# One operand of VectorE's attention products moved to PSUM, z projected alone, a table loaded early and 56 small products ahead of TensorE's list, with every engine's order planned anew

## The chip, the cores and the metric

The kernel runs on one core of a Trainium2 chip. A core has TensorE (matrix products, called PE in the profile, with its weight loads as PEld), VectorE (DVE), ScalarE (ACT), GpSimd (POOL) and SyncE (SP, which issues most loads), on-chip memory SBUF and the accumulator memory PSUM in eight banks. Each engine works through its own list of instructions in order and waits on semaphores for the others. The metric is device time of one execution in microseconds. Before the change it is 243.72 us, the median of three runs (243.62 to 244.6).

## The reference

Four batches of four heads with 1088 positions of 32 features go through linear attention, and the 4352 tokens of 128 features that come out go through a two-layer block. Cut to what is computed:

```python
def phi(x):                                   # S1, S2: 8 x 32
    a = einsum('rd,bhsd->bhsr', S1, x)
    b = einsum('rd,bhsd->bhsr', S2, x)
    return einsum('bhsi,bhsj->bhsij', a, b).reshape(..., 64)
q_p, k_p = phi(q), phi(k)
kv = einsum('bhsf,bhsd->bhfd', k_p, v)
z = sum(k_p, axis=2)
x = einsum('bhsf,bhfd->bhsd', q_p, kv) / (einsum('bhsf,bhf->bhs', q_p, z)[..., None] + 1e-06)
h = tokens(x) @ w_in                          # 128 -> 2048
g = where(h >= 1, h, where(h <= -1, 0, (h + 1) ** 2 / 4))
out = g @ w_out                               # 2048 -> 128
```

S1, S2, w_in and w_out are given in double precision, the rest in single.

## The kernel before

**The two-layer block.** The 4352 tokens are cut in nine chunks of 512 columns (the last has 256), the 2048 inner features in 16 tiles of 128. One chunk and one tile make a unit: 144 of them. `unit(u)` makes h in one PSUM bank by three products (L796 to L798: high part of the weights with high and low part of x, low part with the high part; all in the rounded single format that TensorE takes in one pass), ScalarE makes s = ((h + 1) / 2 clamped at 0) squared (L811, L813), VectorE clamps: g = min(max(h, 1), s) (L816). Then g is split: g_hi is g rounded (a second clamp on VectorE, L816, or a copy on ScalarE, L823, shared out by the table `HI_ACT`), g_lo = g - g_hi is GpSimd's (L827) or, for units that the tables name, VectorE's, with g in a PSUM bank. Three products add the unit to the chunk's accumulator (L837, L838, L841). A "direct" unit (table `FP`) leaves the split out: g itself is multiplied with unrounded weights in one two-pass product (L844). The weights arrive as double-precision words and are rebuilt and split by ScalarE, GpSimd and VectorE (`weights`, `from_double`).

**The attention.** Batch 0 is the front: before its x exists no unit can run. Its k, q and v come first. `keys(0)` projects k (L527), copies to SBUF, forms the products a x b on VectorE or GpSimd (kp, L537), sums them for z (L546), brings z back into the projection's weights as extra columns (L556, L559: the copy into `proj`) and accumulates kv (L567). `queries(0)` projects q with these columns (abq, L656), so that a, b and the share of the denominator come out together; VectorE makes the denominator, its reciprocal, the scaled a (ap) and the products (qp, L682); TensorE turns them (tp, L693), copies bring them to SBUF (qt) and L711 multiplies with kv: nd, of which x_hi and x_lo are made (L443, L444, L723).

Batches 1 to 3 go another way, between the units. `keys(b)`: two banks of projections (abk, L486), two 32 x 32 transposes by VectorE into SBUF (kab, L492), the products kp from kab alone (L505) on VectorE or GpSimd as the table `KP_POOL` says, z (L512), z brought back (L556, L559), kv (L567). `queries(b)`: sixteen products into four banks (abq, L612, with the z columns among the weights), four transposes (qab, L617), all_terms = a x z part (L620), den (L622), the reciprocal (L624), ap (L626), the products qp in three groups (L637, VectorE or GpSimd by `QP_POOL`), their transposes (qt, L642), and gather16 (nd, L737).

**What sets the order.** The program builds a list of steps with a due number, an engine, a cost and the tiles that they read and write; `Plan.run` goes through model time and gives each free engine the step that is due first, holding PSUM banks (`ps`, eight) and SBUF buffers as the table `rings` allows. The result is written out as the order of every engine's list. Until model time `WARM` (24) TensorE's empty places are filled with products of ones (warm, L314 and L315). The numbers at the head of the file (`KEYS`, `QEND`, `FQ`, `I0` and so on) are due numbers and shares.

## Time and profile before

| what | before |
| --- | --- |
| median of three runs | 243.72 us (243.62 to 244.6) |
| the profiled execution | 245.77 us, its span 244.0 us |
| TensorE busy | 231.1 us, 1844 products |
| VectorE busy | 209.0 us, 372 instructions |
| ScalarE busy | 197.2 us, 403 |
| GpSimd busy | 196.3 us, 175 |
| granted TensorE clock, mean | 0.985 |

The span runs from the first to the last instruction. Rows of a timeline are: start in us, length in us, engine, line, operation, what it writes and reads, shape, how many, and in square brackets the idle time before it with what ended it. Rows of a grouped view end with the busy time, the mean length of one in ns, and the idle time before with its causes. Rows of the windows give the stretch, its length, busy time and count of PE, PEld, DVE, ACT and POOL, then the granted TensorE clock, the share of the DMA engines' time and GB/s.

### The profile page before, as it was taken

What the parts mean: (1) busy time and instruction counts of PE and PEld (TensorE: products, weight loads), DVE (VectorE), ACT (ScalarE), POOL (GpSimd) and SP (SyncE); (2) the same over time, 40 slices, a digit from 0 to 9 for tenths busy, and PEclk for the clock granted to TensorE, in tenths of its full rate; (3) what the DMA queues carried; (4) which work ended last, traced back from release to release, by engine and by line L of the source; (5) the groups of instructions that cost most, each with busy time, mean ns of one, the idle gap of its engine ahead of it and who ended that gap; (6) DMA issues with size and microseconds to landing.
All of it is one profiled execution on the core that took longest, in us unless ns stands there. A gap on an engine that the chain in (4) does not pass through costs nothing.

```text
span 244.0 us, 5120 instructions
## 1 busy us (share of the span) xinstructions
PE 231.1 (95%) x1844; PEld 174.7 (72%) x1844; DVE 209.0 (86%) x372; ACT 197.2 (81%) x403; POOL 196.3 (80%) x175
## 2 busy tenths in 40 slices
PE   8879979989999999996999999989999999999994
PEld 3656748757677887574777788767788888888883
DVE  2868889999986999999979999998788588859882
ACT  2548899999989999336588868898899699689993
POOL 5448789997562998986996768999897989969991
PEclk9979999999999999999799999999999999999999
DMA  6971888000001100001000010000100100010001
GB/s 208 415 316 23 261 307 337 6 1 0 0 3 43 43 3 3 0 3 43 3 0 3 0 43 3 1 1 0 47 0 0 42 4 0 1 43 4 0 0 64
DMA packets 4776, 13.88 MB, mean 57 GB/s; under 512 B 528, under 2 KB 784, under 8 KB 4752
## 3 DMA queue, kind: packets, MB, share of 16 engines
q1 hardware_dynamic: 4320, 12.78, 14.4%
q10 hardware_dynamic: 432, 0.79, 0.9%
q8 instruction: 14, 0.23, 0.4%
q14 instruction: 10, 0.08, 0.1%
HBM read 11.34 MB, written 2.23 MB: 56 GB/s over the span
## 4 chain that ended last, share of the span: by engine, by line
PE 61%; DVE 15%; ACT 10%; issue 6%; POOL 5%; DMA 1%; POOLq 0%; ACTq 0%
PE acc L837 9%; PE acc L841 9%; PE acc L838 8%; PE h L796 8%; PE h L797 8%; PE h L798 8%; DVE g L816 5%; ACT s L813 4%; ACT s L811 3%; DVE g_hi L816 3%; POOL g_lo L827 3%; PE acc L844 3%; PE nd L737 2%; POOL kp L505 2%; PE kv L567 2%
## 5 line engine op out<-in xcount | busy, mean ns | idle before, releaser
L827 POOL TENSOR_TENSOR g_lo<-g,g_hi 128x512 fp32r<-128x512 f32 (+1 forms) x128 | 159.0, 1275 | 28.4 <-ACT g_hi L823 12.9
L816 DVE SCALAR_TENSOR_TENSOR g<-h,s 128x512 f32<-128x512 f32 (+1 forms) x135 | 86.1, 649 | 18.4 <-ACT s L813 14.1
L811 ACT ACTIVATE s<-h 128x512 f32<-128x512 f32 (+1 forms) x144 | 78.8, 573 | 15.3 <-PE h L798 12.0
L813 ACT ACTIVATE s<-s 128x512 f32<-128x512 f32 (+1 forms) x144 | 84.7, 614 | 1.8
L816 DVE SCALAR_TENSOR_TENSOR g_hi<-h,s 128x512 fp32r<-128x512 f32 (+1 forms) x91 | 59.2, 654 | 1.7 <-PE acc L838 1.1
L796 PE MATMUL h<-x_hi,wi_hi 128*128 128x512 f32 (+1 forms) x144 | 56.5, 393 | 1.8 <-ACT proj L559 1.3
L797 PE MATMUL h<-x_lo,wi_hi 128*128 128x512 f32 (+1 forms) x144 | 55.1, 383 | 0.0
L798 PE MATMUL h<-x_hi,wi_lo 128*128 128x512 f32 (+1 forms) x144 | 54.9, 381 | 0.0
L837 PE MATMUL acc<-g_hi,wo_hi 128*128 128x512 f32 (+1 forms) x135 | 54.0, 402 | 0.7 <-DVE g_hi L816 0.6
L841 PE MATMUL acc<-g_lo,wo_hi 128*128 128x512 f32 (+1 forms) x135 | 49.0, 393 | 2.3 <-POOL g_lo L827 2.2
L838 PE MATMUL acc<-g_hi,wo_lo 128*128 128x512 f32 (+1 forms) x135 | 51.2, 380 | 0.0
L796 PEld LDWEIGHTS h<-x_hi,wi_hi 128*128 128x128 f32 x144 | 27.1, 189 | 10.0 <-ACT proj L559 1.6
L841 PEld LDWEIGHTS acc<-g_lo,wo_hi 128*128 128x128 f32 x135 | 25.1, 189 | 9.9 <-POOL g_lo L827 3.9
L837 PEld LDWEIGHTS acc<-g_hi,wo_hi 128*128 128x128 f32 x135 | 25.3, 188 | 9.3 <-DVE g_hi L816 2.0
L798 PEld LDWEIGHTS h<-x_hi,wi_lo 128*128 128x128 f32 x144 | 27.2, 189 | 5.5
L797 PEld LDWEIGHTS h<-x_lo,wi_hi 128*128 128x128 f32 x144 | 27.2, 189 | 5.4 <-issue 0.5
L823 ACT CAST g_hi<-g 128x512 fp32r<-128x512 f32 (+1 forms) x44 | 25.4, 582 | 6.7 <-DVE g L816 5.1
L838 PEld LDWEIGHTS acc<-g_hi,wo_lo 128*128 128x128 f32 x135 | 25.4, 188 | 5.1 <-issue 1.0
L505 POOL TENSOR_TENSOR kp<-kab 128x1280 f32<-128x1280 f32 (+1 forms) x4 | 9.9, 2494 | 0.9 <-DVE kab L492 0.9
L844 PE MATMUL acc<-gd,o 128*128 128x512 f32 x18 | 9.1, 598 | 1.1 <-DVE gd L816 1.1
L637 DVE TENSOR_TENSOR qp<-ap,qab 128x768 f32<-128x768 f32 x6 | 9.7, 1611 | 0.1
L642 DVE STREAM_TRANSPOSE qt<-qp 128x768 f32<-128x768 f32 x9 | 8.6, 959 | 0.0
(101 smaller groups left out, 191.1 us busy)
## 6 DMA issues: line engine op xcount, KB each, us to landing
raw_i<-in_w_in SPq DMA_DIRECT2D x4, 512.0 KB, 4.7
raw_o<-in_w_out SPq DMA_DIRECT2D x4, 512.0 KB, 6.6
outT<-o SPq DMA_DIRECT2D x8, 256.0 KB, 2.0
k<-in_kT SPq DMA_DIRECT2D x3, 576.0 KB, 6.6
v<-in_v SPq DMA_DIRECT2D x3, 576.0 KB, 7.6
q<-in_qT SPq DMA_DIRECT2D x3, 576.0 KB, 6.9
k<-in_kT SPq DMA_DIRECT2D x1, 320.0 KB, 3.8
v<-in_v SPq DMA_DIRECT2D x1, 320.0 KB, 6.2
```

The source lines that it names most:

```text
L796: nc.tensor.matmul(t[:, :n], lhsT=wi_hi[:, fj], rhs=x_hi[:, xs], start=True, stop=False)
L797: nc.tensor.matmul(t[:, :n], lhsT=wi_hi[:, fj], rhs=x_lo[:, xs], start=False, stop=False)
L798: nc.tensor.matmul(t[:, :n], lhsT=wi_lo[:, fj], rhs=x_hi[:, xs], start=False, stop=True)
L811: plan.add(u, "ACT", act(n), lambda: nc.scalar.activation(of(s)[:, :n], of(h)[:, :n], AF.Relu, bias=0.5, scale=0.5), r=[h], w=[s])
L813: plan.add(u, "ACT", act(n, False), lambda: nc.scalar.activation(of(s)[:, :n], of(s)[:, :n], AF.Square), w=[s])
L816: nc.vector.scalar_tensor_tensor(out=of(out)[:, :n], in0=of(h)[:, :n], scalar=1.0, in1=of(s)[:, :n], op0=ALU.max, op1=ALU.min)
L823: plan.add(u, "ACT", act(n, False), lambda: nc.scalar.copy(of(g_hi)[:, :n], of(g)[:, :n]), r=[g], w=[g_hi])
L827: plan.add(u, "DVE" if late else "POOL", dve(n) if late else pool_t(n), lambda: eng.tensor_tensor(out=of(g_lo)[:, :n], in0=of(g)[:, :n], i ...
L837: nc.tensor.matmul(of(acc)[:, :n], lhsT=wo_hi[:, fj], rhs=of(g_hi)[:, :n], start=first, stop=False)
L838: nc.tensor.matmul(of(acc)[:, :n], lhsT=wo_lo[:, fj], rhs=of(g_hi)[:, :n], start=False, stop=False)
L841: nc.tensor.matmul(of(acc)[:, :n], lhsT=wo_hi[:, fj], rhs=of(g_lo)[:, :n], start=False, stop=last)
L844: nc.tensor.matmul(of(acc)[:, :n], lhsT=of(whole[j // JW])[:, j % JW * P : (j % JW + 1) * P], rhs=of(g)[:, :n], start=first, stop=last)
```

## The change

1. **One operand in PSUM (batches 1 to 3).** Where VectorE forms kp, ScalarE first copies the b half of kab back into the first projection's PSUM bank, and VectorE reads it there. For the queries the third transpose writes the z part into that bank, where the denominator's product reads it; the reciprocal goes there too, and for groups whose product is VectorE's the scaled a is also written there (per group now, three small products in place of one). The bank is held until the last of these products.
2. **z projected alone.** The queries use the keys' projection weights (eight products into two banks) and four more products into a third bank for the z part, with z's weights in a small tile of their own (`back_z`). The second `proj` tile and the short product of L556 are gone for these batches.
3. **ScalarE's table first.** A copy of 32 columns of ones stands first on ScalarE's list, ahead of the copies that wait for S.
4. **56 tiny products.** They lead TensorE's list (`JUNK`, `count_up`).
5. **The planner** counts TensorE's entries (`rec`), and holds a step back where its model says that the list beyond entry 449 + 256 k is not there yet; the cost of a 32 x 32 transpose is other; all numbers of the tables are other. So the order of every engine's list is another from the first row to the last. There are 12 direct units in place of 9, GpSimd has 121 of the g_lo subtractions in place of 128, VectorE 73 of the g_hi clamps in place of 91 and ScalarE 59 of the copies in place of 44.
6. SBUF places: two small pads, x_hi and x_lo rounded up to whole chunks, and a pool of their own for s, g, g_hi, g_lo and o.

```diff
-FP = (0.24, 0.25, 0.36, 0.36)
+FP = (0.85, 0.78, 0.03, 0)
+JUNK = 56
-KP_POOL = ((0, 2), (1, 0), (1, 1), (2, 1), (3, 0))
+KP_POOL = ((0, 0), (0, 2), (1, 0), (1, 1), (2, 1), (3, 1))
-QP_POOL = ((0, 0), (0, 2), (1, 0), (2, 0), (2, 1))
+QP_POOL = ((0, 0), (1, 0), (1, 1), (1, 2), (2, 1))
-HI_ACT = (0.68, 0.72, 0, 0.27)
+HI_ACT = (0.58, 0.41, 0.49, 0.38)
...
+    HELD, BLOCK = 449, 256
...
+                if e == "PE":
+                    was, told = told, told + s.rec
+                    for k in range((was - self.HELD) // self.BLOCK + 2):
+                        fetched.setdefault(k, now + (6.0 if now < 16 else 2.6))
+                    k = (told - self.HELD) // self.BLOCK
+                    if (was - self.HELD) // self.BLOCK < k:
+                        rest = (told - self.HELD - self.BLOCK * k) / s.rec
+                        cost = max(cost, fetched.setdefault(k, now + 2.6) - now + rest * cost)
...
 def turned32(n):
-    return 0.07 + 0.00116 * n
+    return 0.156 + 0.00105 * n
...
+            if any((b, gi) not in KP_POOL for gi in range(2)):
+                plan.add(d(0.12), "ACT", act(NTL * HR, False), lambda: nc.scalar.copy(
+                    of(abs_[0])[:, : NTL * HR], of(kab)[:, 1].rearrange("p t h i -> p (t h i)")),
+                    r=[kab.part(0), kab.part(1)], w=[abs_[0].part("b")])
...
-                def products(eng=eng, grp=grp, n=n):
+                def products(eng=eng, grp=grp, n=n, pool=pool):
                     x = [of(kab)[:, c, grp[0] : grp[-1] + 1].rearrange("p t h i -> p (t h) i") for c in range(2)]
+                    if not pool:
+                        x[1] = of(abs_[0])[:, grp[0] * HR : (grp[-1] + 1) * HR].rearrange("p (m i) -> p m i", i=R)
...
-            for c0, n in ((0, HR), (HR, R)):
+            for c0, n in ((0, HR), (HR, R))[: 2 if front else 1]:
                 nc.tensor.matmul(of(z)[:, 64 + c0 : 64 + c0 + n], lhsT=back, rhs=of(zm)[:, :n], start=True, stop=True)
 
-        plan.add(d(0.5), "PE", ZB, zback, r=[zm, "back"], w=[z]).mode = 0
-        plan.add(d(0.55), "ACT", act(40), lambda: nc.scalar.copy(
-            proj[b % 2][:, :, 2 * R : 3 * R], of(z)[:, 64 : 64 + HR + R].rearrange("p (h i) -> p h i", i=R)),
-            r=[z], w=[("proj", b % 2)])
+        plan.add(d(0.5), "PE", ZB, zback, r=[zm, "back"], w=[z]).kind(0, 8)
+        if front:
+            plan.add(d(0.55), "ACT", act(40), lambda: nc.scalar.copy(
+                proj[:, :, 2 * R : 3 * R], of(z)[:, 64 : 64 + HR + R].rearrange("p (h i) -> p h i", i=R)),
+                r=[z], w=["proj"])
+        else:
+            plan.add(d(0.55), "ACT", act(HR), lambda: nc.scalar.copy(back_z[:, b % 2], of(z)[:, 64 : 64 + HR]),
+                     r=[z], w=[("back_z", b % 2)])
...
             nm = NTL * H
...
+            abq = [bank(f"abq{b}_{k}") for k in range(2)]
+            cq = bank(f"cq{b}")
+            qab = Buf("kab", f"qab{b}", [P, 2, NTL, H, R])
             den = Buf("dens", f"den{b}", [P, 2 * D, 1])
             ap = Buf("aps", f"ap{b}", [P, nm, R])
...
+            both = [qab.part(0), qab.part(1)]
+            flat = lambda c: of(qab)[:, c].rearrange("p t h i -> p (t h) i")
+            kept = lambda: of(abq[0])[:, : nm * R].rearrange("p (m i) -> p m i", i=R)
+            rec = lambda: of(abq[0])[:, nm * R : nm * (R + 1)].rearrange("p (m i) -> p m i", i=1)
+
+            def project8():
+                for k, rows in enumerate((slice(0, F), slice(F, 2 * F))):
                     for c in quarters:
...
+                        nc.tensor.matmul(of(abq[k])[c, : NTL * D].rearrange("p (t f) -> p t f", f=D),
+                                         lhsT=s_pair[rows, k * D : (k + 1) * D], rhs=of(qb)[rows, :, c],
+                                         start=True, stop=True)
+
+            def project_z():
+                for c in quarters:
+                    nc.tensor.matmul(of(cq)[c, : NTL * D].rearrange("p (t f) -> p t f", f=D),
+                                     lhsT=back_z[:, b % 2], rhs=of(qb)[:, :, c], start=True, stop=True)
+
+            plan.add(d(-0.1), "PE", KPR, project8, r=[qb, "s_pair"], w=abq).kind(2, 32)
+            for k in range(2):
+                plan.add(d(0.0), "DVE", turned32(NTL * D), lambda k=k: nc.vector.transpose(
+                    out=of(qab)[:, :, :, 2 * k : 2 * k + 2].rearrange("p c t h i -> p t c (h i)"),
+                    in_=of(abq[k])[:, : NTL * D].rearrange("p (t c x) -> p t c x", c=2, x=2 * R)),
+                    r=[abq[k]], w=[qab.part(k)])
+            plan.add(d(0.0), "PE", QPR, project_z, r=[qb, ("back_z", b % 2)], w=[cq]).kind(1, 16)
+            plan.add(d(0.1), "DVE", turned32(NTL * D), lambda: nc.vector.transpose(
+                out=of(abq[0])[:, : nm * R], in_=of(cq)[:, : NTL * D]), r=[cq, *both], w=[abq[0].part("c")])
             plan.add(d(0.15), "DVE", dve(nm * R), lambda: nc.vector.tensor_tensor(
...
+                out=all_terms[:, :, :R], in0=flat(0), in1=kept(), op=ALU.mult),
+                r=[*both, abq[0].part("c")], w=["all_terms"])
             plan.add(d(0.2), "DVE", dve(nm * 9), lambda: nc.vector.tensor_reduce(
                 out=of(den)[:, :nm], in_=all_terms, axis=AX.X, op=ALU.add), r=["all_terms"], w=[den])
...
+            plan.add(d(0.25), "DVE", 0.35, lambda: nc.vector.reciprocal(out=rec(), in_=of(den)[:, :nm]),
+                     r=[den], w=[abq[0].part("r")])
             for gi, grp in enumerate(QGRP[b]):
                 d = dues[gi]
                 n = len(grp)
                 g = slice(grp[0] * H, (grp[-1] + 1) * H)
...
                 pool = (b, gi) in QP_POOL
                 eng = nc.gpsimd if pool else nc.vector
+                scaled = (lambda g=g: of(ap)[:, g]) if pool else (lambda g=g: kept()[:, g])
+                tok = ap.part(gi) if pool else abq[0].part(("ap", gi))
+                plan.add(d(0.3), "DVE", dve(n * HR), lambda scaled=scaled, g=g, n=n: nc.vector.tensor_tensor(
+                    out=scaled(), in0=flat(0)[:, g], in1=rec()[:, g].broadcast_to([P, n * H, R]), op=ALU.mult),
+                    r=[*both, abq[0].part("r")], w=[tok])
+                qp = Buf("qp", f"qp{b}_{gi}", [P, 3, H * F])
                 plan.add(d(0.4), "POOL" if pool else "DVE", pool_b(n * H * F) if pool else dve(n * H * F),
...
+                         lambda qp=qp, n=n, g=g, eng=eng, scaled=scaled: eng.tensor_tensor(
                     out=of(qp)[:, :n].rearrange("p t (h i j) -> p (t h) i j", h=H, i=R),
...
+                    in0=scaled().unsqueeze(3).broadcast_to([P, n * H, R, R]),
+                    in1=flat(1)[:, g].unsqueeze(2).broadcast_to([P, n * H, R, R]), op=ALU.mult),
+                    r=[*both, tok], w=[qp])
...
+    plan.add(-44, "ACT", 1.4, lambda: nc.scalar.copy(table, singles[:, :D]), w=["table"])
+
+    def count_up():
+        for _ in range(JUNK):
+            nc.tensor.matmul(of(warm)[:D, :R], lhsT=singles[:, :D], rhs=singles[:, :R], start=True, stop=True)
+
+    plan.add(-60, "PE", 0.05 * JUNK, count_up).kind(0, 4 * JUNK)
```

Three places of the new order. The first is TensorE's list from batch 0's z (`z0`) to its last query product (`abq0`, in four groups; `kv0` is the accumulation of its keys' products, warm are the filling products of ones). Before:

```order
L556 MATMUL z0_196<-zm0_231,back_98 128x32
L556 MATMUL z0_196<-zm0_231,back_98 128x8
L315 LDWEIGHTS const-bfloat16-1.0
L315 MATMUL warm_103<-const-bfloat16-1.0 128x256
L567 MATMUL kv0_240<-kp0_192,v0_112 32x64 x12
L656 MATMUL abq0_1_255<-proj0_99,q0_108 32x96 x8
L656 MATMUL abq0_0_265<-proj0_99,q0_108 32x96 x8
L567 MATMUL kv0_240<-kp0_192,v0_112 32x64 x12
L656 MATMUL abq0_3_294<-proj0_99,q0_108 32x96 x8
L567 MATMUL kv0_240<-kp0_192,v0_112 32x64 x12
L656 MATMUL abq0_2_328<-proj0_99,q0_108 32x96 x12
```

and now:

```order
L584 MATMUL z0_240<-zm0_284,back_102 128x32
L584 MATMUL z0_240<-zm0_284,back_102 128x8
L599 MATMUL kv0_292<-kp0_236,v0_168 32x64 x12
L702 MATMUL abq0_1_307<-proj_103,q0_165 32x96 x8
L702 MATMUL abq0_0_317<-proj_103,q0_165 32x96 x8
L702 MATMUL abq0_3_328<-proj_103,q0_165 32x96 x8
L702 MATMUL abq0_2_343<-proj_103,q0_165 32x96 x12
L599 MATMUL kv0_292<-kp0_236,v0_168 32x64 x12
```

The four groups of query products stand together now, ahead of the second group of kv; ahead of all this the list has the 56 products of ones more.

The second is GpSimd's list where batch 2's queries (`qp2`) and batch 3's keys (`kp3`) come among the units' subtractions (`g_lo`, with the unit's number). Before:

```order
L827 TENSOR_TENSOR g_lo50_1589<-g50_1505,g_hi50_1529 128x512
L505 TENSOR_TENSOR kp3_1607<-kab3_1591 128x1280
L637 TENSOR_TENSOR qp2_0_1631<-ap2_1624,qab2_1556 128x768
L827 TENSOR_TENSOR g_lo51_1648<-g51_1533,g_hi51_1603 128x512
L827 TENSOR_TENSOR g_lo52_1663<-g52_1629,g_hi52_1637 128x512
L637 TENSOR_TENSOR qp2_1_1678<-ap2_1624,qab2_1556 128x768
L827 TENSOR_TENSOR g_lo53_1700<-g53_1661,g_hi53_1668 128x512
```

and now:

```order
L873 TENSOR_TENSOR g_lo50_1599<-g50_1569,g_hi50_1588 128x512
L684 TENSOR_TENSOR qp2_1_1617<-ap2_1610,qab2_1514 128x768
L873 TENSOR_TENSOR g_lo49_1634<-g49_1549,g_hi49_1612 128x512
L873 TENSOR_TENSOR g_lo51_1648<-g51_1603,g_hi51_1629 128x512
L873 TENSOR_TENSOR g_lo52_1677<-g52_1651,g_hi52_1665 128x512
L873 TENSOR_TENSOR g_lo53_1692<-g53_1658,g_hi53_1663 128x512
L873 TENSOR_TENSOR g_lo54_1707<-g54_1675,g_hi54_1682 128x512
L873 TENSOR_TENSOR g_lo55_1721<-g55_1702,g_hi55_1710 128x512
L873 TENSOR_TENSOR g_lo56_1743<-g56_1718,g_hi56_1735 128x512
L533 TENSOR_TENSOR kp3_1766<-kab3_1740 128x1024
L873 TENSOR_TENSOR g_lo57_1785<-g57_1750,g_hi57_1768 128x512
L873 TENSOR_TENSOR g_lo58_1819<-g58_1762,g_hi58_1787 128x512
```

Batch 3's keys stood ahead of batch 2's two query products; now seven units' subtractions lie between, and one of batch 2's query products is left on GpSimd in place of two.

The third is ScalarE's list where batch 1's z goes back into the projection's weights (`proj1` before, `back_z` now; s are the units' two passes). Before:

```order
L811 ACTIVATE s4_647<-h4_581 128x512
L425 CAST wi_hi_89<-magi1_497 128x512
L813 ACTIVATE s4_647<-s4_647 128x512
L811 ACTIVATE s5_663<-h5_625 128x512
L559 COPY proj1_100<-z1_448 128x5x8
L811 ACTIVATE s6_674<-h6_641 128x512
L813 ACTIVATE s5_663<-s5_663 128x512
```

and now:

```order
L465 COPY qt0_413<-tp0_2_0_509 128x384
L592 COPY back_z_104<-z1_481 128x32
L465 COPY qt0_413<-tp0_2_1_522 128x384
L415 ACTIVATE mago1_553<-raw_o1_338 128x512
L447 CAST wo_hi_95<-o32_0_551 128x512
L465 CAST x_hi_97<-nd0_2_0_555 128x3x64
L465 CAST x_hi_97<-nd0_3_0_572 128x2x64
L465 CAST x_hi_97<-nd0_3_1_574 128x64
L857 ACTIVATE s0_612<-h0_582 128x512
```

The copy of z stands ahead of the first unit's s now (s0), and between the sixth and the seventh unit's before (s5, s6).

139 lines of the change are left out of this document (61 added, 78 removed).

## The prediction

> **What bounds the kernel now.** I read the page's busy times first, then TensorE's timeline row by row for starts that lie too far apart, then what the late engine did just before each of them.
>
> ```profile
> span 244.0 us, 5120 instructions
> PE 231.1 (95%) x1844; PEld 174.7 (72%) x1844; DVE 209.0 (86%) x372; ACT 197.2 (81%) x403; POOL 196.3 (80%) x175
> ...
> 84.75 0.39 PE L796 MATMUL h<-x_hi,wi_hi 128*128 128x512 f32 x1
> ...
> 88.91 0.39 PE L796 MATMUL h<-x_hi,wi_hi 128*128 128x512 f32 x1
> ```
>
> TensorE sets the time. From 84.75 to 88.91 lie three units' worth of work, 18 wide products in 4.16 us: 0.231 us from start to start. The busy figure of 95% hides the idle time, since a matmul's modelled length (0.39) is longer than its pitch. The 144 units need six products each (the last 16 at half width): (128 x 6 + 16 x 3) x 0.231 = 188 us. So some 56 us of the span are the start, the attention work of batches 1 to 3 on TensorE, the end, and gaps. The gaps show in the timeline:
>
> ```profile
> 31.30 0.40 PE L841 MATMUL acc<-g_lo,wo_hi 128*128 128x512 f32 x1
> 32.96 0.50 PE L796 MATMUL h<-x_hi,wi_hi 128*128 128x512 f32 x1 [1.26 <-ACT proj L559]
> ...
> 52.38 0.39 PE L841 MATMUL acc<-g_lo,wo_hi 128*128 128x512 f32 x1
> 53.84 1.13 PE L844 MATMUL acc<-gd,o 128*128 128x512 f32 x2 [1.07 <-DVE gd L816]
> ...
> 113.24 0.39 PE L798 MATMUL h<-x_hi,wi_lo 128*128 128x512 f32 x1
> 115.85 0.50 PE L841 MATMUL acc<-g_lo,wo_hi 128*128 128x512 f32 x1 [2.22 <-POOL g_lo L827]
> ...
> 161.20 0.40 PE L838 MATMUL acc<-g_hi,wo_lo 128*128 128x512 f32 x1
> 162.23 0.50 PE L837 MATMUL acc<-g_hi,wo_hi 128*128 128x512 f32 x1 [0.63 <-DVE g_hi L816]
> ```
>
> Start to start less 0.23 leaves 1.43, 1.23, 2.38 and 0.80 us: 5.8 us in the four largest. The start has one more, in the chain of waits; the windows show what it and the gap at 113 do to the clock:
>
> ```profile
> 9.14 0.39 PE z L556 x4
> ...
> 11.13 0.32 PE abq L656 x15
> 11.45 2.16 issue
> 13.61 0.24 PE abq L656
> ```
>
> ```profile
> 0.00:7.00 7.00, 5.59 (x96) 2.68 (x99) 1.78 (x8) 2.54 (x9) 3.65 (x21) 1.00 0.67 233
> 0.00:11.50 11.50, 10.04 (x221) 6.32 (x222) 6.01 (x16) 4.44 (x14) 5.76 (x23) 1.00 0.82 306
> 15.00:20.00 5.00, 5.00 (x77) 3.12 (x76) 3.65 (x12) 3.00 (x10) 2.59 (x3) 0.68 0.38 155
> 110.00:120.00 10.00, 7.78 (x56) 5.63 (x58) 9.97 (x14) 6.35 (x11) 8.06 (x7) 0.86 0.07 26
> ```
>
> At 11.45 TensorE stops for 2.16 us in the middle of the first batch's query products and waits for nothing that the profile shows. After each long gap the granted clock falls: 0.68 over 15 to 20, 0.86 over 110 to 120. That is (1 - 0.68) x 5 = 1.6 us and (1 - 0.86) x 10 = 1.4 us of lost TensorE time, if TensorE is what counts there.
>
> **The change, part by part: VectorE's products.** Here is why VectorE is late in the middle:
>
> ```profile
> L637 DVE TENSOR_TENSOR qp<-ap,qab 128x768 f32<-128x768 f32 x6 | 9.7, 1611 | 0.1
> L617 DVE STREAM_TRANSPOSE qab<-abq 128x288 f32<-128x288 f32 x12 | 4.9, 457 | 0.0
> L620 DVE TENSOR_TENSOR all_terms<-qab 128x288 f32<-128x288 f32 x3 | 3.4, 1124 | 0.0
> L505 DVE TENSOR_TENSOR kp<-kab 128x1024 f32<-128x1024 f32 x1 | 3.4, 3355 | 0.0
> L505 DVE TENSOR_TENSOR kp<-kab 128x1280 f32<-128x1280 f32 x1 | 2.4, 2357 | 0.0
> L537 DVE TENSOR_TENSOR kp<-ab,abk 128x768 f32<-128x768 f32 x2 | 1.8, 951 | 2.4 <-ACT ab L532 2.4
> ...
> 42.70 1.93 DVE L637 TENSOR_TENSOR qp<-ap,qab 128x768 f32<-128x768 f32 x1
> 145.39 0.94 DVE L637 TENSOR_TENSOR qp<-ap,qab 128x768 f32<-128x768 f32 x1
> 108.12 3.35 DVE L505 TENSOR_TENSOR kp<-kab 128x1024 f32<-128x1024 f32 x1
> ...
> 42.37 3.43 POOL L827 TENSOR_TENSOR g_lo<-g,g_hi 128x512 fp32r<-128x512 f32 x2 [0.30 <-DVE g_hi L816]
> 145.61 1.88 POOL L827 TENSOR_TENSOR g_lo<-g,g_hi 128x512 fp32r<-128x512 f32 x1 [2.15 <-DVE g_hi L816]
> ```
>
> The same 768-wide product from two SBUF tiles takes 0.94 us when it begins while GpSimd is idle (145.39) and 1.93 when GpSimd is already in its own two-operand subtraction (42.37); the subtraction that begins at 145.61 then takes 1.88. They take turns. The front's product of the same size with one operand in PSUM (L537) takes 0.95 beside a busy GpSimd. That is the form that the change gives batches 1 to 3. Counted on VectorE: five query products at 0.95 in place of six at 1.61 (4.8 for 9.7); two key products, both 1280 wide, at 0.95 x 1280 / 768 = 1.6 in place of 2.36 and 3.36 (3.2 for 5.7); nine transposes in place of twelve (-1.4); three denominators' products at about 0.45 in place of 1.12 (-2.0). Together 11 us less on VectorE. Eighteen fewer copies of g_hi stand on its list as well, fifteen of them taken by ScalarE, which has room (81%), and GpSimd has seven fewer subtractions. ScalarE's two new copies into PSUM stand beside those products, off TensorE's path; uncovered, they would cost their own length.
>
> What that is worth is read from the gaps. At 113 the order before put two key and query products of GpSimd's ahead of the g_lo that TensorE waits for, while VectorE held a 3.35 us product; in the new order batch 3's keys stand seven subtractions after batch 2's one query product. At 52 the direct unit's g waits behind VectorE's query product and the weights; in the new order batch 1's three query products are all GpSimd's and the units beside them skip its subtraction. At 31, the copy of batch 1's z stands behind the first units' instructions on ScalarE; in the new list it stands before the first unit. So all four causes are taken away: 5.8, and 1.4 of clock, is 7.2 us. But the whole list of every engine is planned anew, so others come late in turn. Bounds: all 7.2 gained; or all lost again at other places (0), or worse (a rival below). I take 4.0, a little over half, since the work behind three of the four gaps has really shrunk.
>
> **TensorE's own work.** Two rows for a query's projection and a 64-row projection, two for a direct unit:
>
> ```profile
> 36.08 0.77 PE L612 MATMUL abq<-q,proj 32*32 32x288 f32 x32
> 95.24 0.71 PE L486 MATMUL abk<-k,s_pair 64*32 64x288 f32 x16
> ...
> 49.44 1.02 PE L844 MATMUL acc<-gd,o 128*128 128x512 f32 x2
> 50.53 0.39 PE L796 MATMUL h<-x_hi,wi_hi 128*128 128x512 f32 x1
> ```
>
> The sixteen products (0.77) become eight like L486 (0.71) and four for z, 8 passes: between a quarter of 0.77 (0.19) and half of 0.71 (0.36). I take 0.28: +0.22 for each of three batches, 0.65. A direct unit: from 49.44 to 50.53 lie its two passes and one L841, 1.09 - 0.23 = 0.86 against 3 x 0.231 = 0.69. There are 12 in place of 9: +0.5. Sum +1.1 us.
>
> **The front.** Ahead of the gap TensorE had run 221 products and 222 weight loads. Code comes by queue:
>
> ```profile
> q8 instruction: 14, 0.23, 0.4%
> ...
> 4.45 1.28 ACT L875
> ...
> 5.12 1.21 PE L527 MATMUL abk<-s_all,k 128*32 128x64 f32 x72 [0.16 <-DMA k<-in_kT]
> ...
> 21.65 0.47 PE L796 MATMUL h<-x_hi,wi_hi 128*128 128x512 f32 x1
> 24.27 0.50 PE L796 MATMUL h<-x_hi,wi_hi 128*128 128x512 f32 x1
> ```
>
> Fourteen packets of 16 KB for 3688 entries are about 256 entries each. So I read the gap as: the first 443 or so entries were there, the next block was asked for one block earlier, at entry 190 or so (195 by 7.00), and came 6.6 us later among the loads. The 56 products put 224 entries in front (each runs as two passes with a load). Entry 190 then passes near 3 us, if a pass costs what abq's do (0.32 / 15 = 21 ns, 112 passes 2.4 us); the far bound is zback's 0.39 / 4 = 98 ns, 11 us. I take 3 us for all, by the nearer row: covered, since TensorE's first real product waited for k until 5.12. The block would then be there by 9 or 10, about when z's last product ended before (9.14 + 0.39). The next boundary, 256 entries on, falls after all of the first batch's query products, so a second pause there (again up to 2 us) holds up transposes and batch 1's keys, and no longer VectorE's chain on the query products. Preloading the table takes up to 1.28 us off ScalarE's path ahead of z; it makes good a pause that now falls just there, and I count nothing more for it. Units run without a break from 24.27, one (0.7) came earlier: 23.6 in effect. Gain: at most the gap and the clock, 2.2 + 1.6 = 3.8; at least 0, if the pause only moves on. I take 1.5.
>
> The Trainium skill, "Runtime: NRT & Kernel Launch", section "Instruction fetch mechanics", speaks against this part: TensorE's buffer is to hold 2048 instructions, refilled in blocks of 256, with the fetch hidden. The block size agrees with the 16 KB packets; the buffer does not agree with a stop near entry 443. By that rule the 56 products would be useless, the front would gain nothing, and the sum would be 1.5 us higher.
>
> **Sum.** The profiled execution took 245.77 with a span of 244.0; the median of the runs shown is 243.72, so I subtract from the median: -4.0 (gaps) + 1.1 (TensorE) - 1.5 (front) = -4.4, 239.3 us.
>
> **The rivals.** *Everything holds*: the gaps stay closed (-7.2) and the front gains 2.5: 243.7 - 7.2 + 1.1 - 2.5 = 235.1. For it: VectorE and GpSimd both lose work where they were full. Against: a long order rarely has no gap. *The gaps come back elsewhere*: gaps 0, the front -1.5, TensorE +1.1, and about 1 us of VectorE's relief: 242.3. For it: four gaps of the old order were not planned either. *The pause is not code, or moves on at full length*: the front 0 and the rest as forecast, 240.8. *Slower: banks.* The first projection's PSUM bank is now held from the projection until VectorE's last product of that batch, where a bank was free after the transposes; batch 3's products stand spread over some 27 rows of VectorE's list, 14 units or so. The gap at 31 is a wait of this kind: a unit's first product waits for a tile that a late copy reads. If each of some 25 units in batches 2 and 3 waits 0.25 us for its bank (a quarter of one 0.95 product on VectorE), that is 6.2 us, and 243.7 - 4.4 + 6.2 = 245.5; it decides from 0.18 us a unit (4.4 / 25). Against it: the order is written with the number of banks known.
>
> **Chances.** Forecast 0.45, everything holds 0.15, gaps back 0.18, pause stays 0.08, banks 0.14. Half a per cent is 1.2 us, about what a measurement of this kernel can tell from no change: faster means under 242.5. Of the gaps-back case 0.09 is faster, 0.07 same, 0.02 slower; of the forecast 0.43 is faster and 0.02 same; of the pause case 0.01 is same; the banks are slower but for 0.01. So faster 0.74, same 0.11, slower 0.15. Range 235.5 to 244.2: it leaves out the lower half of the second case and most of the banks. The likeliest case alone is 237.5 to 241.
>
> **What would show it.** Right: the 768-wide VectorE products near 0.95 with little spread; no gap over 1 us on TensorE between 30 and 165; the long "issue" before abq gone or after the last abq; the second unit before 23. Wrong: "issue" as long as before among the query products, or abk beginning after 6 (the small products are dear); first products of units that wait for a clamp or copy while batch 2 or 3 holds its bank; GpSimd late on g_lo after batch 1's three products in a row.

## The result, and the profile after

The changed kernel takes 238.17 us (median of four runs, 238.15 to 238.38); the kernel before, in four runs, 244.05. The ratio is 0.976, its 95% interval 0.9736 to 0.9784. Forecast were 239.3 us and a range of 235.5 to 244.2. The size is close, but one of its three terms, the front, came out with the wrong sign, as the profile shows at once.

The head of the page after, and two of the windows that were read before the change:

```profile
span 236.4 us, 5229 instructions
PE 229.7 (97%) x1912; PEld 178.3 (75%) x1912; DVE 191.9 (81%) x361; ACT 202.0 (85%) x418; POOL 183.5 (78%) x167
...
15.00:20.00 5.00, 3.39 (x82) 2.38 (x71) 4.11 (x18) 3.14 (x11) 3.40 (x4) 1.00 0.47 166
110.00:120.00 10.00, 10.00 (x112) 7.18 (x113) 10.00 (x17) 8.79 (x18) 9.72 (x8) 1.00 0.07 26
```

VectorE has 17 us less work, the granted clock no longer falls (0.68 and 0.86 before in these windows), and 110 to 120 is full of products: 112 instead of 56. In TensorE's timeline one gap is left where there were four of 0.8 to 2.4 us:

```profile
30.03 0.39 PE L844 MATMUL h<-x_hi,wi_lo 128*128 128x512 f32 x1
31.11 0.50 PE L887 MATMUL acc<-g_lo,wo_hi 128*128 128x512 f32 x1 [0.70 <-POOL g_lo L873]
```

Start to start less 0.23 that is 0.85 us; before the four were 5.8 together. VectorE's groups, by form, are near the forecast (0.95, 1.6 and 0.45): 0.94 us for the 768-wide product with one operand in PSUM, 1.48 for the 1280-wide one, 0.44 for the denominator's.

```profile
L684 DVE TENSOR_TENSOR qp<-abq,qab 128x768 f32<-128x768 f32 x5 | 4.7, 943 | 0.1
L533 DVE TENSOR_TENSOR kp<-kab,abk 128x1280 f32<-128x1280 f32 x2 | 3.0, 1480 | 0.0
L664 DVE TENSOR_TENSOR all_terms<-qab,abq 128x288 f32<-128x288 f32 x3 | 1.3, 444 | 0.0
```

The front went the other way:

```profile
0.83 6.12 PE L909 MATMUL warm<-const-float32-1.0 128*32 128x8 f32 x112 [0.83 <-PEq L1000]
...
8.49 1.51 PE L555 MATMUL abk<-s_all,k 128*32 128x64 f32 x48
...
13.35 1.69 PE L702 MATMUL abq<-proj,q 128*32 128x96 f32 x72
14.85 0.51 PE L599 MATMUL kv<-kp,v 128*32 128x64 f32 x22
16.97 0.30 PE L599 MATMUL kv<-kp,v 128*32 128x64 f32 x2 [1.61 <-issue]
...
25.97 0.50 PE L842 MATMUL h<-x_hi,wi_hi 128*128 128x512 f32 x1
```

The 56 products take 6.12 us (55 ns a pass), the first keys' product starts at 8.49 instead of 5.12, and the units run without a break from 25.97 instead of 24.27. An entry is one row of TensorE's list, a product's pass or a weight load. The boundary near entry 449, where the kernel before stopped, is passed at 12.10 without a pause; its packet of code started at 8.61 instead of 11.22. The pause that is left, 1.61 us of "issue", comes at the next boundary, at entry 701, behind the last abq and no longer among them. Last, the products themselves are closer together. The first and the last row of one stretch of unit products before, and of one after:

```profile
172.54 0.49 PE L841 MATMUL acc<-g_lo,wo_hi 128*128 128x512 f32 x1
205.42 0.39 PE L838 MATMUL acc<-g_hi,wo_lo 128*128 128x512 f32 x1
```

```profile
168.77 0.49 PE L887 MATMUL acc<-g_lo,wo_hi 128*128 128x512 f32 x1
197.51 0.39 PE L887 MATMUL acc<-g_lo,wo_hi 128*128 128x512 f32 x1
```

143 products in 32.88 us are 0.230 us each, 126 in 28.74 are 0.228. Over all neighbouring starts of 512-wide products between 50 and 200 us the means are 230.2 and 227.6 ns.

### The profile page after: what moved, and what is told of

It reads as the page before. It is cut to its first block, busy times and chain, and to the rows that moved or that the text cites. A ratio compares the mean times of both kernels' runs of the same rounds, so it can differ in the third digit from the quotient of the medians.

```text
span 236.4 us, 5229 instructions
## 1 busy us (share of the span) xinstructions
PE 229.7 (97%) x1912; PEld 178.3 (75%) x1912; DVE 191.9 (81%) x361; ACT 202.0 (85%) x418; POOL 183.5 (78%) x167
## 4 chain that ended last, share of the span: by engine, by line
PE 87%; ACT 6%; issue 2%; DMA 2%; DVE 1%; ACTq 0%
PE acc L887 12%; PE acc L883 12%; PE h L842 12%; PE acc L884 12%; PE h L843 12%; PE h L844 12%; PE warm L909 3%; ACT s L857 2%; ACT s L859 2%; PE nd L783 2%; DMA raw_i<-in_w_in 2%; PE kv L599 2%; PE acc L890 1%; PE warm L334 1%; PE tp L739 1%
## 5 line engine op out<-in xcount | busy, mean ns | idle before, releaser
L873 POOL TENSOR_TENSOR g_lo<-g,g_hi 128x512 fp32r<-128x512 f32 (+1 forms) x121 | 147.3, 1245 | 27.4 <-ACT g_hi L869 12.2
L862 DVE SCALAR_TENSOR_TENSOR g<-h,s 128x512 f32<-128x512 f32 (+1 forms) x132 | 84.3, 652 | 23.3 <-ACT s L859 19.9
L842 PE MATMUL h<-x_hi,wi_hi 128*128 128x512 f32 (+1 forms) x144 | 58.3, 405 | 0.1
L883 PE MATMUL acc<-g_hi,wo_hi 128*128 128x512 f32 (+1 forms) x132 | 50.8, 386 | 0.0
L862 DVE SCALAR_TENSOR_TENSOR g_hi<-h,s 128x512 fp32r<-128x512 f32 (+1 forms) x73 | 47.2, 648 | 2.7 <-PE acc L884 1.5
L887 PE MATMUL acc<-g_lo,wo_hi 128*128 128x512 f32 (+1 forms) x132 | 46.8, 387 | 0.7 <-POOL g_lo L873 0.7
L869 ACT CAST g_hi<-g 128x512 fp32r<-128x512 f32 (+1 forms) x59 | 34.7, 598 | 2.8 <-DVE g L862 2.7
L890 PE MATMUL acc<-gd,o 128*128 128x512 f32 x24 | 11.9, 591 | 0.0
L862 DVE SCALAR_TENSOR_TENSOR gd<-h,s 128x512 f32<-128x512 f32 x12 | 8.0, 682 | 1.3 <-ACT s L859 1.0
L533 POOL TENSOR_TENSOR kp<-kab 128x1024 f32<-128x1024 f32 (+1 forms) x4 | 8.2, 2073 | 0.1
```

The source lines that it names most:

```text
L842: nc.tensor.matmul(t[:, :n], lhsT=wi_hi[:, fj], rhs=x_hi[:, xs], start=True, stop=False)
L862: nc.vector.scalar_tensor_tensor(out=of(out)[:, :n], in0=of(h)[:, :n], scalar=1.0, in1=of(s)[:, :n], op0=ALU.max, op1=ALU.min)
L869: plan.add(u, "ACT", act(n, False), lambda: nc.scalar.copy(of(g_hi)[:, :n], of(g)[:, :n]), r=[g], w=[g_hi])
L873: plan.add(u, "DVE" if late else "POOL", dve(n) if late else pool_t(n), lambda: eng.tensor_tensor(out=of(g_lo)[:, :n], in0=of(g)[:, :n], i ...
L883: nc.tensor.matmul(of(acc)[:, :n], lhsT=wo_hi[:, fj], rhs=of(g_hi)[:, :n], start=first, stop=False)
L887: nc.tensor.matmul(of(acc)[:, :n], lhsT=wo_hi[:, fj], rhs=of(g_lo)[:, :n], start=False, stop=last)
```

## The experiments

The kernel before ran beside all of them; each ratio is to that. Twelve kernels ran, in three sets of four, each set on another chip (the kernel before: 243.43, 243.98 and 244.34 us). Kernels of different sets are therefore compared by their ratios and profiles, and a difference of a few tenths of a microsecond between sets says nothing.

### The 56 small products left out

```diff
-        for _ in range(JUNK):
+        for _ in range(0):
```

> The changed kernel, same order, with the 56 small products left out (the output is not touched by them). Read from the changed kernel's timeline: they hold TensorE for 6.12 us at half clock, the first keys' product starts at 8.49 instead of 5.12, and the full clock comes at 10.0. Theory A, they cost more than they save: without them abk starts near 5.1, the code pause comes back among the query products at about 2.2 us as it was before the change, and the units run from about 24.3 instead of 25.97: 236.5 to 237.2 us. Theory B, they pay (a pause behind the last query product is worth more than the 3.4 us at the start): 238.2 or slower, up to 239.5.

234.73 us, ratio 0.9646 (0.9598 to 0.9695): 3.4 us faster than with them. Theory B falls, and A was right about the cost but wrong about the pause:

```profile
5.24 1.51 PE L555 MATMUL abk<-s_all,k 128*32 128x64 f32 x48 [2.75 <-DMA k<-in_kT]
...
11.49 1.69 PE L702 MATMUL abq<-proj,q 128*32 128x96 f32 x72
12.99 0.70 PE L599 MATMUL kv<-kp,v 128*32 128x64 f32 x24
...
23.33 0.50 PE L842 MATMUL h<-x_hi,wi_hi 128*128 128x512 f32 x1
```

There is no pause among the 72 query products, although nothing stands in front now. The new order has them in one piece ahead of the second group of kv, and counted in entries the boundary near 449 falls some eight products behind them. There the 24 products of kv take 0.70 us instead of 0.51 to 0.54, and that is all that is left of the pause at this boundary. The new order alone had taken the boundary out of the query products; the small products had nothing left to do. The units start 2.64 us earlier, and the gap at 30.03 (0.85 us) is gone too.

### Two ways of making them cheaper

One weight column instead of 32 (*thin*), and nine wide fillers ahead of 53 of them (*wide first*; the line that takes out its three wide fillers behind the small ones is not shown):

```diff
-            nc.tensor.matmul(of(warm)[:D, :R], lhsT=singles[:, :D], rhs=singles[:, :R], start=True, stop=True)
+            nc.tensor.matmul(of(warm)[:1, :R], lhsT=singles[:, :1], rhs=singles[:, :R], start=True, stop=True)
```

```diff
+        for _ in range(9):
+            nc.tensor.matmul(of(warm), lhsT=ones[:, :P], rhs=ones, start=True, stop=True)
-        for _ in range(JUNK):
+        for _ in range(JUNK - 3):
```

> The 56 small products load one column of weights instead of 32, same number of entries, same order. Theory A, their 55 ns per pass is the load of 32 columns at half clock: they then take 1.5 to 3 us, the first keys' product starts when k arrives (near 5.1 to 5.5), and the end comes 2 to 3 us earlier: 235.3 to 236.3 us. Theory B, a pass has a fixed length at half clock whatever its width: 56 products again 6.1 us and the time again 238.2 within 0.4. Theory C, they get cheap but the pause, asked for at the same entries but now earlier, meets the loads: the pause moves in front of the query products and eats most of it, 237.0 to 238.0.

> Nine 512-wide filling products stand first, then 53 of the small ones (as many entries ahead of the keys as in the changed kernel, whose three wide fillers behind the small ones go). Theory A, the clock sets the small products' length: full clock comes near 4.5, the small ones then take about 27 ns per pass, 2.9 us, the first keys' product starts near 7.5 (8.49 in the changed kernel) and runs at full clock (1.2 us for 72 passes instead of about 2.2): 1 to 2 us gained, 236.2 to 237.2. Theory B, 55 ns per pass is fixed: the small ones take 5.8 us, the first keys' product starts at 10 or later, 239 us or more.

Thin: 238.08 us (0.9783, 0.9734 to 0.9832). Wide first: 238.77 (0.9814, 0.9765 to 0.9863). TensorE's front of each:

```profile
0.84 2.95 PE L909 MATMUL warm<-const-float32-1.0 128*1 128x8 f32 x112 [0.84 <-PEq L1000]
...
5.59 1.51 PE L555 MATMUL abk<-s_all,k 128*32 128x64 f32 x48 [0.20 <-DMA k<-in_kT]
...
16.06 0.30 PE L599 MATMUL kv<-kp,v 128*32 128x64 f32 x2 [3.10 <-issue]
```

```profile
4.69 3.60 PE L911 MATMUL warm<-const-float32-1.0 128*32 128x8 f32 x106
...
8.55 1.51 PE L555 MATMUL abk<-s_all,k 128*32 128x64 f32 x48
```

A pass takes 26 ns with one column (2.95 / 112) and 55 with 32, both before the full clock, so about half of it was the weight load; with the nine fillers ahead it takes 34 ns (3.60 / 106), at full clock. Thin starts the keys at 5.59, and yet ends where the changed kernel does: the pause, at the same two products, grew from 1.61 to 3.10 us. It still ends 0.91 us earlier than in the changed kernel, and the clock takes that back: from 17.76 the granted clock is 0.50 for 3.41 us, where it does not fall in the changed kernel. Theory C is nearest, but the pause stands behind the query products, not ahead of them. In the trace the instruction packet that ends it starts at 13.67 (14.56 in the changed kernel), 4.1 us after TensorE crossed the boundary before it at about 9.6, while the loads move 413 GB/s. Most of what was won in front of the boundary was waited for at the next.

Wide first shows a second cost. Its windows:

```profile
4.00:8.00 4.00, 4.00 (x106) 3.31 (x105) 0.31 (x2) 0.81 (x5) 0.51 (x3) 1.00 1.04 411
8.00:11.00 3.00, 3.00 (x96) 2.71 (x95) 0.52 (x1) 1.08 (x4) 1.11 (x1) 0.50 1.06 413
```

TensorE is never idle from 4 to 8, but its work is the small products, and from 8 to 11 the granted clock is half: in this run the small products did not keep the clock up. So the keys begin at 8.55, at half clock. The changed kernel agrees: it is busy with small products from 0.83, and its full clock is granted from 10.02, 3.1 us after its first wide filler (6.88); here the wide fillers begin at 0.84 and the full clock comes at 4.56. (The windows print 1.00 for the time before the first grant too; that the clock is half there is read from the wide fillers, 0.43 us each, where 512-wide products later take 0.23.)

### Wide fillers in their place

Ten 512-wide fillers until k is there, as before the change, and the fourteen narrow fillers of the wait for z as seven wide ones (only the first is shown):

```diff
...
-        for _ in range(JUNK):
-            nc.tensor.matmul(of(warm)[:D, :R], lhsT=singles[:, :D], rhs=singles[:, :R], start=True, stop=True)
+        for _ in range(7):
+            nc.tensor.matmul(of(warm), lhsT=ones[:, :P], rhs=ones, start=True, stop=True)
```

> The kernel without the small products (234.73 us) with seven more 512-wide filling products at the start, ten in all as before the change, and the fourteen 256-wide fillers in the wait for z as seven of 512, so the number of entries ahead of the query products stays the same to within two. Without them TensorE stood idle from 2.4 to 5.24 and had the full clock only from 9.82, so the keys' products and the wait for z ran at half clock. Theory A, the clock is what the front still loses: full clock near 4.5, query products from about 9.9 instead of 11.49, and since the boundary at entry 449 stays just behind them a pause of about 1 us may stand there, beside VectorE's work on the queries: 0.5 to 1.5 us gained, 233.2 to 234.2. Theory B, the block of code is what counts: it was asked for near 7 us and came at 13.2, will come no sooner, and everything behind the query products starts as late as now: 234.5 to 235.0.

234.48 us (234.06 to 235.16, six runs), ratio 0.959 (0.9548 to 0.9631): the lowest time of all, and faster than the kernels before and after, though not told apart from the kernel without small products.

```profile
9.91 1.69 PE L704 MATMUL abq<-proj,q 128*32 128x96 f32 x72
...
12.71 0.47 PE L601 MATMUL kv<-kp,v 128*32 128x64 f32 x17 [1.01 <-issue]
...
19.00 0.44 PE L741 MATMUL tp<-ident,qp 128*128 128x128 f32 x2 [1.07 <-issue]
...
22.96 0.50 PE L844 MATMUL h<-x_hi,wi_hi 128*128 128x512 f32 x1
```

The clock does its part: the query products start at 9.91 instead of 11.49. Then two pauses of 2.1 us together follow, and the units start only 0.37 us earlier. The time lies between the ranges of the two theories; by what holds the front up it is theory B, the code's arrival.

### The small products out of the planner too

```diff
-JUNK = 56
+JUNK = 0
```

> The changed kernel with the small products taken out of the planner too, so that the planner knows where the entries stand, fills the start with wide products itself and makes a new order from the same numbers. Theory A, the front is now planned for what happens and gains at the code pauses (1.01 and 1.07 us in the kernel with ten wide fillers): 233.0 to 234.3. Theory B, the numbers were fitted to the order with the products in it; moved by 2 us, other steps meet, and a gap over 1 us between 25 and 165 takes it back: 235 to 240.

237.44 us (0.9724, 0.9696 to 0.9751), where leaving the same products out of the program alone gave 234.73 (0.9646).

```profile
8.53 0.54 PE L599 MATMUL kv<-kp,v 128*32 128x64 f32 x24 [1.79 <-DMA v<-in_v]
...
11.96 1.26 PE L702 MATMUL abq<-proj,q 128*32 128x96 f32 x49
14.53 0.70 PE L702 MATMUL abq<-proj,q 128*32 128x96 f32 x23 [1.31 <-issue]
...
24.31 0.48 PE L842 MATMUL h<-x_hi,wi_hi 128*128 128x512 f32 x1
```

B in its size, but most of the loss is in the front, not in a later gap over 1 us: this plan puts kv ahead of the query products, where it waits 1.79 us for v, and the pause is back among them. The units start 0.98 us later than without small products, and one gap of 0.71 us stands at 28.28, behind a g_hi of VectorE's. The good order of the front came out of a plan that counted 56 products which the program is better without.

### VectorE's operands back in SBUF

```diff
-                    if not pool:
-                        x[1] = of(abs_[0])[:, grp[0] * HR : (grp[-1] + 1) * HR].rearrange("p (m i) -> p m i", i=R)
-                scaled = (lambda g=g: of(ap)[:, g]) if pool else (lambda g=g: kept()[:, g])
+                scaled = lambda g=g: of(ap)[:, g]
```

> The changed kernel and its order, but VectorE's five query products and two key products of batches 1 to 3 read both operands from SBUF (the scaled a stays in SBUF; the copy of b into PSUM is still made and not read; the result is the same). Theory A, the shared port was what closed the gaps: the 768-wide products go from 0.94 to between 0.94 and 1.9 by what GpSimd does beside them, the 1280-wide ones from 1.48 to 2.4 or more, 4 to 6 us more on VectorE and as much lost on GpSimd; at least one gap over 1 us comes back on TensorE around 95 to 120, and the time is 239.5 to 242. Theory B, the new order alone closes them (VectorE has some 40 us without work in the span): within 0.5 us of 238.2 although the products are as long as before.

240.37 us (0.9864, 0.9832 to 0.9895), 2.2 us more than the changed kernel in the same order. The worst place, first in this kernel and then the same place after the change (VectorE's timeline), and what it does to TensorE here:

```profile
117.00 3.11 DVE L531 TENSOR_TENSOR kp<-kab 128x1280 f32<-128x1280 f32 x1
120.04 0.17 DVE L577 TENSOR_TENSOR zm<-z,blocks 128x32 f32<-128x32 f32 x1
```

```profile
117.05 1.47 DVE L533 TENSOR_TENSOR kp<-kab,abk 128x1280 f32<-128x1280 f32 x1
118.44 0.18 DVE L579 TENSOR_TENSOR zm<-z,blocks 128x32 f32<-128x32 f32 x1
```

```profile
118.90 0.40 PE L882 MATMUL acc<-g_hi,wo_lo 128*128 128x512 f32 x1
120.27 0.41 PE L582 MATMUL z<-zm,back 128*128 128x32 f32 x2 [0.97 <-DVE zm L577]
```

The same product beside the same work of GpSimd takes 3.11 us from SBUF and 1.47 with one operand in PSUM; zm is 1.6 us late and TensorE stops for 1.14. Two gaps of 0.5 us stand at 107.7 and 157.1 besides, 2.2 us in all; the gap at 30 is 0.5 us shorter here, and the spans differ by 2.0. VectorE's seven products take 3.2 us more (10.9 for 7.7), less than the 4 to 6 expected. Theory A.

### Code and numbers apart

The changed code without small products, with the planner's numbers of before; and the code before with the new numbers. "Code" here includes the planner's own: its count of entries, its rule for holding a step back and its cost of a transpose, none of which was tried apart:

```diff
-KEYS = {1: (-39.71, -34.52), 2: (-19.83, -13.39), 3: (-40.51, -38.71)}
+KEYS = {1: (-37.58, -17.56), 2: (-19.74, -15.52), 3: (-44.29, -36.91)}
 ... and so on for every number and table at the head of the file
```

> The changed code (one operand in PSUM, z alone, table first, new places in SBUF) with no small products and with the planner's due numbers, shares and tables of the kernel before; only the costs of the new operations stay. Theory A, the code itself closes the gaps (11 us less on VectorE): no TensorE gap over 1 us between 30 and 165 and 234 to 237 us. Theory B, the new numbers close them: at least two gaps over 1 us stay there, and 238.5 to 242 us.

> The kernel before with all due numbers, shares and tables of the changed one, its own code and costs (VectorE reads both operands from SBUF, sixteen query products, no small products, the old places in SBUF). It fills the fourth corner beside old code with old numbers (243.98), new code with old numbers and no small products (243.97) and new code with new numbers and no small products (234.5 to 234.7). Theory A, the new numbers carry the gain and the PSUM operand adds the 2.2 us that taking it away cost: 237 to 240. Theory B, code and numbers only fit together: VectorE, with 1.6 us or more per 768-wide product and more clamps in the first half, falls behind, gaps over 1 us come back: 241.5 to 246.

| | old numbers | new numbers |
| --- | --- | --- |
| old code | 243.98 | 247.96 (ratio 1.0148, 1.0121 to 1.0174) |
| new code, no small products | 243.97 (ratio 0.9989, 0.9954 to 1.0023) | 234.73 (0.9646); 237.44 (0.9724) when they are out of the plan too |

Neither half gains anything, one loses, and together they are worth 3.5% (ratio 0.9646). The planner counted the 56 products only in that kernel; where it counts none, as in the other corners, the two together are worth 2.8%. By the gaps it is theory B in both; both times lie above its ranges. With the old numbers the new code's products are as short as they should be, and this happens:

```profile
L684 DVE TENSOR_TENSOR qp<-abq,qab 128x768 f32<-128x768 f32 x6 | 5.6, 938 | 0.0
...
60.44 0.39 PE L844 MATMUL h<-x_hi,wi_lo 128*128 128x512 f32 x1
63.29 0.50 PE L842 MATMUL h<-x_hi,wi_hi 128*128 128x512 f32 x1 [2.47 <-DVE qp L684]
```

A unit's first product waits for a bank that VectorE still reads, and TensorE stands for 2.62 us: the prediction's rival of the banks, in an order that was not made for the change. (A second gap, 1.82 us at 29.1, waits for a g_hi.) With the new numbers the old code's products are as long as ever:

```profile
L637 DVE TENSOR_TENSOR qp<-ap,qab 128x768 f32<-128x768 f32 x5 | 8.0, 1615 | 0.0
...
12.66 0.54 PE L567 MATMUL kv<-kp,v 128*32 128x64 f32 x24 [0.76 <-issue]
...
117.12 3.22 DVE L505 TENSOR_TENSOR kp<-kab 128x1280 f32<-128x1280 f32 x1
...
120.44 0.87 PE L567 MATMUL kv<-kp,v 128*32 128x64 f32 x24 [2.16 <-issue]
```

Its front is good, with the pause behind the query products at 0.76 us and no small product in the program (a second one, 1.19 us, stands at 19). But TensorE stands for 2.16 us before kv at 120.44. The profile calls that "issue", and yet it is no wait for code: the entry is 2177 and not near a boundary, no packet of instructions lands between 103 and 121, and kv reads the kp that VectorE's 1280-wide product from two SBUF tiles finishes at 120.34. From 119.78 the granted clock is 0.50 for 6.83 us. Eight gaps of 0.3 to 0.8 us that wait for VectorE stand between 55 and 166 besides. So the old code loses with the new numbers by its long products, as theory B had it.

### Places in SBUF, and the table

```diff
-            pool = ps if b.tag == "ps" else wide if b.tag in ("s", "g", "g_hi", "g_lo", "o") else sb
+            pool = ps if b.tag == "ps" else sb
-    cst.tile([P, 32], F32, name="pad0")
-    XC = -(-(NT + 64) // CH) * CH
+    XC = NT + 96
```

All three edits without the small products (first), XC alone beside the wide fillers (second), and the reverse of them, as far as there was room, in the kernel before (third: pad, pool and a longer x_hi). The changed kernel has one such pad, not two:

> The kernel without the small products (234.73 us, 512-wide products 0.2268 to 0.2300 us from start to start between 50 and 200 us) with the places in SBUF as before the change: no pad, x_hi and x_lo 96 columns longer than the tokens and not rounded up, and s, g, g_hi, g_lo and o in the common pool. Same instructions, same order. Theory A, the places in SBUF set the pitch (0.2283 to 0.2323 before the change): it goes back to near 0.231 and the time to 236.2 to 237.2. Theory B, the pitch fell for lack of VectorE's and GpSimd's work beside it: pitch and time stay, 234.4 to 235.2.

> The kernel without small products and with ten wide fillers (234.48 us), only the length of x_hi and x_lo put back to 96 columns over the tokens, so that x_lo starts 160 columns earlier; pad and pool stay. Theory A, the start of x_lo alone makes the products that read it slow: they go from 228 to 232 ns from start to start, the others stay near 227.5, and 144 of them cost 0.6 us: 234.9 to 235.3. Theory B, the pool or the pad made the difference: all pitches stay within 1 ns and the time within 0.3 us.

> The kernel before with the changed kernel's places in SBUF for what stands up to x_lo and for s, g, g_hi, g_lo and o: the small pad, x_hi 160 columns longer so that x_lo starts a whole number of 512-column chunks after it, and the pool of their own. Same instructions and order. Theory A, the place of x_lo and the other tiles sets the pitch: the products that read x_lo go from 232 to near 227.5 ns from start to start, the others from 229.5 to near 228, and the time falls by 1 to 2 us: ratio to the kernel before 0.992 to 0.996. Theory B, the pitch in the kernel before came from its own traffic of VectorE and GpSimd: ratio 0.998 to 1.002 and the pitch as it was.

First: 235.3 us (0.9618, 0.9573 to 0.9663). Second: 235.34 (0.9629, 0.9598 to 0.9659). They are 0.6 and 0.9 us above their bases (234.73 and 234.48), each in another set; the times and intervals do not tell them apart, and by its ratio the first is not above its base. The pitch, the time from one start to the next, does differ. The same 126 products of the same order with the wide fillers, and then with XC put back:

```profile
164.93 0.50 PE L889 MATMUL acc<-g_lo,wo_hi 128*128 128x512 f32 x1
193.63 0.39 PE L889 MATMUL acc<-g_lo,wo_hi 128*128 128x512 f32 x1
```

```profile
165.84 0.49 PE L889 MATMUL acc<-g_lo,wo_hi 128*128 128x512 f32 x1
194.79 0.39 PE L889 MATMUL acc<-g_lo,wo_hi 128*128 128x512 f32 x1
```

28.70 and 28.95 us, 227.8 and 229.8 ns each. Over all neighbours between 50 and 200 the products that read x_lo have 232.8 and 232.9 ns with the old length of x and 227.6 to 227.8 with the new one; the others differ by 1.3. From 45 to 195 us the two kernels lose some 0.7 us each on their bases by this. So far theory A. But the third run, 244.03 us (0.9992, 0.9969 to 1.0016), has x_lo where the changed kernel has it and still 234.6 ns for these products, 230.7 over all. Where x_lo starts is therefore not enough; which of the tiles that lie behind it matters was not tried.

The table:

```diff
-    plan.add(-44, "ACT", 1.4, lambda: nc.scalar.copy(table, singles[:, :D]), w=["table"])
+    plan.add(-44, "ACT", 1.4, lambda: None, w=["table"])
```

> The kernel without the small products (234.73 us), its first ScalarE instruction left out too, so that the 1.28 us load of ScalarE's table stands in front of the first copy that waits for S, at 4.4. Theory A, covered: the copies of S end by 6.2, before the first keys' product of batch 0 (from 5.24 at half clock) needs a copy, and the time stays within 0.4 of 234.73. Theory B, it holds up ScalarE's first copy of the keys' projection and with it z and the query products, by up to 1.3 us: 235.3 to 236.0.

234.5 us (0.9595, 0.9547 to 0.9644) without it: no difference. But the edit did not do what was expected of it. ScalarE's list here:

```profile
2.82 1.28 ACT L927 ACT_TABLE_LOAD   x1 [2.82 <-POOL blocks L347]
```

The load runs at 2.82 without the copy too (2.81 with it), ahead of the wait for S, which lasts until 4.32; in the kernel before it ran at 4.45, behind that wait. So the copy of ones is not what moved the load. What a load at 4.45 would cost the changed kernel was not measured, and neither theory was tried.

## Why the prediction was right, and where it was not

The found values are start to start on TensorE, from the two profiled executions (spans 244.0 and 236.4).

| term | forecast | found |
| --- | --- | --- |
| the four large gaps | -4.0 for gaps and clock, of 7.2 | -5.0 |
| clock at 110 to 120 | in the line above | -1.4 |
| five smaller gaps (0.3 to 0.5 us each) | not counted | -1.8 |
| z projected alone | +0.65 | +1.3 |
| direct units, 12 for 9 | +0.5 | +0.5 |
| front | -1.5 | +1.7 |
| pitch of the wide products | not counted | -1.9 |
| sum | -4.4 | -6.6 of the spans' -7.6 |

The clock's share is one of the execution that was profiled: executions of the kernel before with a mean granted clock of 1.000 took 242.7 to 243.7 us, those at 0.990 to 0.993 243.7 to 245.0, and the profiled one (0.985) 245.77. The gap of 0.33 us at 118.77, one of the five, lies in the stretch at half clock and is in part counted twice. Of the spans' difference 1.0 us has no term.

**The middle** was right in its mechanism and too small: the four gaps closed, and the smaller ones with them; one of 0.85 us came at 30.03. VectorE's rows came out near the forecast lengths. One reading behind them was weaker than the prediction has it: of the two front products said to take 0.95 "beside a busy GpSimd", GpSimd stood idle beside the one at 6.7. The changed kernel's five products settle it, all between 0.92 and 0.96. That the shorter products are needed was shown twice: 2.2 us without them in the same order, and a wait of 2.16 us behind one long product in the old code with the new numbers. So was that they don't do it alone: with the old numbers the time did not change.

**z alone** was under-sized. The prediction took 0.28 us for z's four products, "between a quarter of 0.77 and half of 0.71". Start to start they take 0.49 to 0.62:

```profile
141.12 0.72 PE L646 MATMUL abq<-q,s_pair 64*32 64x288 f32 x16
141.77 0.69 PE L652 MATMUL cq<-q,back_z 128*32 128x288 f32 x8
142.39 0.50 PE L883 MATMUL acc<-g_hi,wo_hi 128*128 128x512 f32 x1
```

The three projections take 1.13 to 1.27 us with z, where the sixteen products took 0.70 to 0.83. Eight passes of 128 rows cost about what sixteen of 64 rows do (0.62 and 0.65): as if half-height passes ran two at a time and full-height ones did not, which was not tried apart.

**The front** failed at the forecast's "if a pass costs what abq's do" (21 ns). It cost 55, so that the products take 6.12 us where 3 were taken as covered, and the forecast's own sign of it, abk beginning after 6, came true (8.49); the second unit started at 25.97 and not before 23. Two reasons were shown: the weight load (26 ns with one column) and the missing clock (34 ns at full clock). What separates 34 from abq's 21 was not tried: abq's passes load 32 columns too, but go to four parts of a bank in turn, where the small ones write the same place each time. The far bound, 11 us, did hold the cost. The second step came out as the forecast has it: the block for entry 449 is there by 9.64 (forecast 9 or 10), and the next boundary brings a second pause behind the query products. What the forecast left out is that the new order needs none of this: without the small products the boundary lies behind the query products as well. That the pause is a wait for code stands: its place moves with the count of entries, and TensorE goes on 1.4 to 1.5 us after a 16 KB instruction packet has landed, in the kernel before (packet from 11.22 for 0.94 us, product at 13.61) as after it (14.56, 0.97, 16.97). The Trainium skill's "Runtime: NRT & Kernel Launch", section "Instruction fetch mechanics", has the fetch mostly hidden behind a buffer of 2048 instructions; here the measurement decides, with pauses of 0.5 to 3.1 us near entry 449 or 705 in both kernels and in all of the others but the one without small products (at most 0.3).

So the forecast is near the result because errors cancel: the front 3.2 us worse than forecast and z 0.7, the middle and the pitch together 6.1 us better (in the median, where less of the clock was lost before, some 4). The pitch was in no term of the forecast: that part is luck.

**The rivals.** Everything holds (235.1) is near what the change gives without its small products (234.73), but not for its reasons: its front gained 0.9 us there (units from 23.33 instead of 24.27) and not 2.5, and the pitch gave 1.9 that the rival did not have. The banks never held up the changed kernel; their price is seen with the old numbers. The Trainium skill's "TensorE: Matmul & The Clock Gate", section "LDWEIGHTS (loading the stationary operand)", makes a weight load's length follow its columns: by its formula 31 columns more are some 26 ns, an estimate. The trace agrees, with 29 ns between the passes of one column (26) and of 32 (55). It would not have told the forecast's 21 ns apart, since abq's passes load 32 columns as well.

## What to carry to other kernels

Work that is added only to shift something else must be priced as it will run there: at the clock of that moment, with its own weight loads, and against a run without it. A faster instruction gains where the order is made for it: the new code and the new numbers were worth nothing or less apart, and 7 to 9 us together. When a plan is fitted to an assumption, try the program without what was assumed and keep the plan. An edit that is to take a thing away is checked in the trace, as the table load shows; and a wait that the profile cannot name is checked against what the waiting product reads, as the 2.16 us before kv show.

## What the hardware showed that was not expected

- Small products (eight columns) keep TensorE busy in the profile but not its clock: 106 such passes ran without a break from 4.69, and from 7.97 the granted clock was 0.50 for 3.4 us.
- A code pause grew when the front got faster: 1.61 us with the slow small products, 3.10 with the fast ones, at the same boundary (entries 701 and 700).
- The places of tiles in SBUF changed the pitch of wide products by 2 ns (227.6 against 229.5), for those that read x_lo by 5, some 0.7 us of 234.5. Which tile's place does it stayed open.
- A 1280-wide VectorE product from SBUF took 3.11 us beside GpSimd's work, and 1.47 with one operand in PSUM.
